# Sliding-window attention and routed experts on one core: transposing k and q on TensorE in place of through DRAM, with the routing rows loaded earlier in a half step

## The chip, the cores and the metric

The kernel runs on one core of one Trainium2 chip. A core has five engines that run their own instruction lists in order and meet at semaphores: TensorE (PE; its weight loads are listed apart as PEld), VectorE (DVE), ScalarE (ACT), GpSimd (POOL) and SyncE (SP). POOL and SP issue the transfers here, which 16 DMA engines carry out. The metric is the device time of one execution in microseconds (us); lower is better.

## The reference

q, k and v have 8 batches of 8 heads of 576 rows of 64 numbers. The attention is causal, looks 128 positions back, and has a bias that grows linearly with the distance (ALiBi). Its output is read as 4608 tokens of 512 numbers and goes through 8 experts, of which every token takes all, weighted by a matrix P that eight rounds of row and column scaling (Sinkhorn) have balanced.

```python
scores = scale * q @ k.T;  scores = where(mask, scores + bias, -1e9)
x = softmax(scores) @ v                      # -> (4608, 512)
P = exp(x @ w_gate - max)                    # (4608, 8), then 8 rounds:
P /= P.sum(1); P /= P.sum(0); P *= N / E
out = sum over e of P[:, e:e+1] * (relu(x @ w1[e]) @ w2[e])
```

## The kernel before, in words

The order of every engine's instructions is written out by hand: each engine executes its part of the program in the order in which the Python code emits it, and nothing is rescheduled.

**Attention (lines 158 to 559).** The unit of work is a block: one batch b and one of five stretches kb of 128 key positions (the fifth has 64). A loop over 40 blocks (line 510) emits, for each block: scores of four heads (`scores`, line 255: matmuls at L280 into the PSUM tile psS, and the exponential on ACT at L291), the gate logits of finished tokens (L358), the turning of a finished block of x (`put_x`, L373 on PE, L382 on DVE), pieces of expert 0's matmuls as filling (`fill`: L129 first layer, L147 second layer), the mask (L301, DVE), then scores of the other four heads, and `attend` for the block before (L333 on PE, L341 and L342 on DVE). The first dozen blocks follow a list of operations (`ORDER`, line 51). psS has one buffer at this stage, so the scores of one half wait for the exponential of the half before.

The scores need q and k with the head dimension on the partitions. There are two ways to that here:
- *By TensorE.* `load_qk` (line 193) loads half of a batch's heads as 96 partitions by 4 by 384 numbers (L208, POOL). `turn` (line 226) reorders it on DVE (L230, 96x1536). `tr_unit` (line 236) makes one of four units: six transposing matmuls of 96x96 (L241) into one PSUM bank psT of the pool "pmm", which has four banks and serves also the filling, the gates and `put_x`; then one copy out of it (L250, 128x576), on ACT for k and on DVE for q. In the block loop, the turns for batch b+1 are made in blocks kb 0 and 2 of batch b, and the units in blocks kb 1 to 4: k's in the first half of the block and q's after the filling in the second half.
- *By DMA.* For the pairs in `by_dma` (line 187: k of batches 4 to 7, q of batches 5 and 7) POOL copies the tensor, cast to 16 bits, to DRAM (L196), and SP transposes it from there into KT or QT (L519), in block kb 1 of the batch before. These pairs have no turns and no units.

**Between (lines 561 to 671).** P is balanced on DVE and POOL while PE works on the rest of expert 0. P's transpose goes to DRAM (PTd, L668).

**Experts 1 to 7 (lines 674 to 1170).** A task is one expert and one group of 512 tokens; there are 63. Each half step h of the loop at line 1017 does the second layer of task h and the first layer of task h+1, both as seven products in place of eight (Strassen), whose sums are on DVE. DVE scales the x of task h+2 by its routing row (`make_xs`, L704) in half step h. The row of a task is read from PTd into 128 partitions, 256 KB, by `load_p` (L696); x is read by `load_x` (L123), 512 KB; both are issued by SP, and both have two buffers. `load_next(h)` (line 1011) issues the row and the x of task h+3, in this order, at the end of half step h. In the half steps of expert 1 (h from 0 to 7) SP also issues two stores (L633, listed at L85) that wait for ACT in the middle of the half step.

Of the kernel before, what the change touches and what calls it, by code (L numbers as in the profile page):

```python
# [9 lines left out]
FP16 = mybir.dt.float16  # L10
# [4 lines left out]
def kernel(  # L15
# [10 lines left out]
    nc = tc.nc  # L26
# [4 lines left out]
    B, H, S, Dh = q.shape  # L31
    HD = H * Dh
# [125 lines left out]
    with (  # L158
# [7 lines left out]
        def new_banks(name: str, n: int):  # L166
# [13 lines left out]
        KTs = [asb.tile([P, NPR, S], FP16, name=f"KT{i}") for i in range(2)]  # L180
        QTs = [asb.tile([P, NPR, S], FP16, name=f"QT{i}") for i in range(2)]
# [1 line left out]

        raw: dict = {}


        by_dma = {("k", b) for b in range(4, B)} | {("q", b) for b in range(5, B, 2)}
        d16 = {
            nb: nc.dram_tensor(f"{nb[0]}16_{nb[1]}", [S, HD], FP16, kind="Internal").ap()
            for nb in sorted(by_dma)  # L190
        }

        def load_qk(b: int):
            for nm, src in (("k", k), ("q", q)):
                if (nm, b) in by_dma:
                    nc.gpsimd.dma_start(  # L196
                        out=d16[nm, b].rearrange("s (h d) -> s h d", d=Dh),
                        in_=src[b].rearrange("h s d -> s h d"),
                    )
            for half in range(2):  # L200
                h0 = 4 * half
                for nm, src in (("k", k), ("q", q)):
                    if (nm, b) in by_dma:
                        continue
                    t = asb.tile(
                        [RP, 4, RT * Dh], FP16, name=f"{nm}f_{b}_{half}", tag="qkf", bufs=6
                    )
                    nc.gpsimd.dma_start(  # L208
                        out=t,
                        in_=src[b, h0 : h0 + 4].rearrange("h (p r) d -> p h (r d)", r=RT),  # L210
                    )
                    raw[(nm, b, half)] = t
# [202 lines left out]
        with tc.manual_schedule():  # L415
            new_banks("aps", 2)
            zw = asb.tile([P, GT], FP16, name="zw")
            nc.vector.memset(zw, 0.0)

            def warm():  # L420

                z = aps.tile([P, GT], FP32, name="psZ", tag="psN")
                nc.tensor.matmul(out=z, lhsT=zw[:, 0:P], rhs=zw)

            nc.sync.dma_start(out=ident, in_=ident_h.ap())
            load_qk(0)
            nc.sync.dma_start(out=rel, in_=rel_h.ap())
            for h in range(H):
                nc.scalar.mul(sid[:, h, :], ident, -float(slopes[h]) / scale)

            def make_mask(h):
                if h < H:
                    nc.scalar.activation(
                        out=maskT[:, h, :], in_=rel, func=AF.Exp, scale=-float(slopes[h])
                    )

            for vsb in vsbs:
                nc.vector.memset(vsb[:, :, :, Dh : Dh + 2], 1.0)
            load_v(0)
            nc.gpsimd.dma_start(  # L440
                out=wg_sb, in_=moe_w_gate.rearrange("(dt p) e -> p dt e", p=P)
            )
            load_qk(1)
            load_w1(0, per, 2)
            load_v(1)
            load_w2(0, per)

            blocks = [(b, kb) for b in range(B) for kb in range(NKB)]
            pts: dict = {}
            groups = 0  # L450
            def finish(i: int):
                b, kb = blocks[i]
                return attend(b, kb, pts[i], pts[i - 1] if kb > 0 else None)

            def finish2(i: int):
                nonlocal groups
                b, kb = blocks[i]
                put_x(b, kb, xsbs.pop(i))
                done = b * S + min(S, (kb + 1) * P)
                while (groups + 1) * GT <= done:  # L460
                    nc.sync.dma_start(
                        out=x_dram(groups), in_=xT[:, :, GT * groups : GT * groups + GT]
                    )
                    if groups in (NHI // 4, NHI // 4 + 1):
                        load_x(f"0_{groups}", groups)
                    add_group(groups)
                    groups += 1
                return done

            xsbs: dict = {}  # L470
            masks: dict = {}

            def op(name: str):

                c, n = name[0], [int(x) for x in name[1:].split(".") if x]
                if c == "B":
                    new_banks(f"aps_{len(masks)}", n[0])
                elif c == "z":
                    warm()
                elif c == "e":  # L480
                    make_mask(n[0])
                elif c == "v":
                    load_v(n[0])
                elif c == "l":
                    load_qk(n[0])
                elif c in "tT":
                    turn(n[0], n[1], "k" if c == "t" else "q")
                elif c in "uU":
                    tr_unit(n[0], "k" if c == "u" else "q", *n[1:])
                elif c == "s":  # L490
                    pt, mask = scores(*blocks[n[0]], n[1])
                    masks[tuple(n)] = mask
                    pts[n[0]] = (*pts.get(n[0], ()), pt)
                elif c == "m":
                    masks[tuple(n)]()
                elif c == "n":
                    xsbs[n[0]] = finish(n[0])
                elif c == "x":
                    return finish2(n[0])
                elif c == "g":  # L500
                    gates((n[0] + 1) * P)
                elif c == "f":
                    moe.pop(0)[1]()
                return 0

            done = 0
            for name in ORDER:
                done = max(done, op(name))
            first_i = max(xsbs, default=-1) + 2
            for i, (b, kb) in enumerate(blocks):  # L510
                if i < first_i:
                    continue
                units = []
                if kb >= 1 and b + 1 < B:
                    units = [(b + 1, n, kb - 1) for n in ("k", "q") if (n, b + 1) not in by_dma]
                if kb == 1:
                    for nm, t in (("k", KTs), ("q", QTs)):
                        if (nm, b + 1) in by_dma:
                            nc.sync.dma_start(  # L519
                                out=t[(b + 1) % 2], in_=d16[nm, b + 1], transpose=True  # L520
                            )
                credit = min(credit + RATE, 6.0) if groups else 0.0
                pt0, mask0 = scores(b, kb, 0)
                gates(done)
                done = finish2(i - 2)
                for u in units[: len(units) // 2]:
                    tr_unit(*u)
                fill(1)
                turning = kb in (0, 2) and b < B - 1
                if turning and ("k", b + 1) not in by_dma:  # L530
                    turn(b + 1, kb // 2, "k")
                mask0()
                pt1, mask1 = scores(b, kb, 1)
                pts[i] = (pt0, pt1)
                xsbs[i - 1] = finish(i - 1)
                mask1()
                fill(2)
                for u in units[len(units) // 2 :]:
                    tr_unit(*u)
                fill(1)  # L540
                if turning and ("q", b + 1) not in by_dma:
                    turn(b + 1, kb // 2, "q")
                if kb == 0 and b + 1 < B:
                    load_v(b + 1)
                if kb == 3 and b + 2 < B:
                    load_qk(b + 2)
            i = len(blocks) - 1
            credit = 1e9
            fill(1)
            xsbs[i] = finish(i)  # L550
            gates(done)
            done = finish2(i - 1)
            fill(1)
            fill(1)
            done, last = finish2(i), done
            gates(last)
            fill(1)
            gates(done)
            fill(1 << 20)
# [7 lines left out]
    with (  # L567
# [17 lines left out]
        for it in range(ITERS):  # L585
# [3 lines left out]
                out=P_sb,  # L589
# [420 lines left out]

        def load_next(h):
            if h + 3 < NT:
                load_p(h + 3)
                load_x(h + 3, tasks[h + 3][1])

        load_next(-1)
        for h in range(NT + 1):
            j = h + 1
            slot = -1

            def extra():
                nonlocal slot
# [178 lines left out]
```

## Time and profile before

| what | value |
|---|---|
| time, median of three runs | 1011.35 us (1010.64, 1011.35, 1013.1) |
| time of the profiled execution | 1010.64 us |
| span of the profiled execution | 1008.9 us (1.7 us less: start and end around the span) |
| PE busy | 988.7 us, 98% of the span |
| PE weight loads busy | 802.6 us, 80% |
| DVE busy | 809.1 us, 80% |
| ACT busy | 642.0 us, 64% |
| POOL busy | 219.1 us, 22% |
| granted TensorE clock, mean | 0.999 |

Batch b of the attention is taken here from the start of its first scores to that of the next batch's: 48.0, 72.0, 94.5, 115.7, 136.8 and 158.0 us are the starts of batches 2 to 7. Expert 0 and the balancing last to about 222 us, and experts 1 to 7 to the end.

How to read it: busy times are sums over instructions that overlap in the engine's pipeline, so a busy PE is not a PE at its peak. A line of the timeline has start, length, engine, source line, operation, output<-inputs, shape and count; lines with a count merge neighbours. What stands in brackets is the engine's idle time before it and the instruction that ended it. In the view of waits a line says who waited for whom, the sum in us, how often, and the longest.

### The profile page before, as it was taken

Reading aid. Unit: us, or ns where it says so; the run is one execution under the profiler, and the core shown is the slowest. Engines: PE = TensorE matmul, PEld = TensorE weight load, DVE = VectorE, ACT = ScalarE, POOL = GpSimd, SP = SyncE. Lnnn points to the kernel's source line nnn. Section 1 sums busy time; section 2 is a strip of 40 time slices with the busy share of each in tenths; the row PEclk is TensorE's granted clock in tenths of the full one; section 3 lists DMA queues with packets and bytes.
Section 4 is the critical chain, followed back from the end, with each engine's and each line's share of the span. In section 5 each row is a group of like instructions: output and inputs, shape, how many; then the busy total and the mean of one; then the engine's idle time right before and its main releaser. Section 6 shows DMA issues by size and latency. Waiting matters only on the chain. (4 is left out here: it accounts for less than half of the span.)

```text
span 1008.9 us, 22248 instructions
## 1 busy us (share of the span) xinstructions
PE 988.7 (98%) x9101; PEld 802.6 (80%) x9101; DVE 809.1 (80%) x1252; ACT 642.0 (64%) x1177; POOL 219.1 (22%) x218
## 2 busy tenths in 40 slices
PE   6999999999999999999999999999999999999997
PEld 4655454458888788888888888888888888888886
DVE  4776665578999898878889988888889988888886
ACT  5866666558999766655656666656566565665652
POOL 7424410201322311111111211111112112222222
PEclk9999999999999999999999999999999999999999
DMA  9999991482987874444446766443438546555546
GB/s 167 198 156 137 139 147 64 102 189 77 228 160 152 180 146 102 104 101 101 101 101 138 140 140 130 95 96 95 95 95 159 117 102 147 145 139 137 136 95 136
DMA packets 163894, 130.87 MB, mean 130 GB/s; under 512 B 85680, under 2 KB 141776, under 8 KB 163792
## 3 DMA queue, kind: packets, MB, share of 16 engines
q0 software_dynamic: 117728, 60.58, 46.3%
q1 hardware_dynamic: 45744, 68.61, 22.8%
q8 instruction: 71, 1.16, 0.5%
q10 hardware_dynamic: 320, 0.26, 0.1%
q14 instruction: 31, 0.25, 0.1%
HBM read 112.90 MB, written 20.20 MB: 132 GB/s over the span
## 5 line engine op out<-in xcount | busy, mean ns | idle before, releaser
L129 PEld LDWEIGHTS <-w1t_122 128*128 128x128 f16 x288 | 25.7, 98 | 26.2 <-issue 0.9
L764 PEld LDWEIGHTS <-w1t_3049 128*128 128x128 f16 x288 | 28.2, 98 | 4.5
L764 PEld LDWEIGHTS <-w1t_3067 128*128 128x128 f16 x288 | 28.1, 98 | 4.6 <-issue 1.2
L764 PEld LDWEIGHTS <-w1t_8191 128*128 128x128 f16 x288 | 28.1, 98 | 4.3 <-issue 0.3
L764 PEld LDWEIGHTS <-w1t_4989 128*128 128x128 f16 x288 | 28.1, 98 | 3.8 <-issue 0.3
L764 PEld LDWEIGHTS <-w1t_7655 128*128 128x128 f16 x288 | 28.2, 98 | 3.6 <-issue 0.3
L764 PEld LDWEIGHTS <-w1t_10591 128*128 128x128 f16 x288 | 28.2, 98 | 3.6 <-issue 0.3
L764 PEld LDWEIGHTS <-w1t_3807 128*128 128x128 f16 x256 | 25.0, 98 | 2.9
L219 POOL DMA_DIRECT2D vsb_79<-in_v_dram x20 | 17.1, 864 | 36.8 <-PE psN_1_1093 L333 7.0
L219 POOL DMA_DIRECT2D vsb_80<-in_v_dram x20 | 16.9, 849 | 29.1 <-PE psT_q_2_2239 L241 4.6
L280 PEld LDWEIGHTS <-KT_76 64*128 64x128 f16 (+1 forms) x160 | 5.5, 96 | 13.8 <-issue 12.5
L280 PEld LDWEIGHTS <-KT_75 64*128 64x128 f16 (+1 forms) x160 | 5.3, 97 | 14.1 <-issue 13.0
L597 POOL PARTITION_ALL_REDUCE ca_sb<-cs_sb x8 | 3.1, 390 | 60.5 <-DVE cs_sb L594 60.5
L639 ACT ACTIVATE acc_lo<-acc_lo,Pe_sb 128x512 f32<-128x512 f32 (+1 forms) x24 | 14.8, 616 | 0.0
L85 POOL DMA_DIRECT2D out_dram<-acc_lo x12 | 13.3, 1498 | 0.0
L358 PEld LDWEIGHTS <-xT 128*128 128x128 f16 x144 | 6.1, 96 | 5.1 <-issue 2.9
L892 POOL DMA_DIRECT2D acc_lo<-st_1_0_3650 x1 | 1.2, 1243 | 34.1 <-ACT st_1_0_3650 L891 34.1
L764 PEld LDWEIGHTS <-ws_2_4125 128*128 128x128 f16 x72 | 7.0, 98 | 1.5 <-issue 0.7
L764 PEld LDWEIGHTS <-ws_1_3369 128*128 128x128 f16 x72 | 7.0, 97 | 1.3
L85 POOL DMA_DIRECT2D out_dram<-acc_hi x6 | 5.7, 1561 | 9.7 <-DVE acc_hi L882 9.7
L919 DVE TENSOR_TENSOR acc_lo<-acc_lo 128x512 f32<-128x512 f32 x12 | 7.7, 682 | 0.0
L764 PEld LDWEIGHTS <-ws_2_3961 128*128 128x128 f16 x72 | 7.0, 98 | 0.8
(4097 smaller groups left out, 3534.1 us busy)
## 6 DMA issues: line engine op xcount, KB each, us to landing
xTd<-xT SPq DMA_DIRECT2D x9, 512.0 KB, 4.9
out_dram<-acc_lo SPq DMA_DIRECT2D x12, 256.0 KB, 5.6
vsb_79<-in_v_dram POOLq DMA_DIRECT2D x16, 128.0 KB, 6.7
vsb_80<-in_v_dram POOLq DMA_DIRECT2D x16, 128.0 KB, 6.6
out_dram<-acc_lo SPq DMA_DIRECT2D x12, 128.0 KB, 4.0
out_dram<-acc_lo POOLq DMA_DIRECT2D x12, 128.0 KB, 7.4
w1t_122<-in_moe_w_dram POOLq DMA_DIRECT2D x2, 512.0 KB, 10.3
w2t_130<-in_moe_w_dram POOLq DMA_DIRECT2D x1, 1024.0 KB, 14.0
```

Source lines behind the costliest of these rows:

```text
L85: eng.dma_start(out=out[t0 : t0 + n, c0:c1], in_=t[n * c : n * c + n], **kw)
L129: nc.tensor.matmul(out=psh, lhsT=w1t[:, dt, P * ft : P * ft + P], rhs=x[:, dt, :], start=(dt == 0), stop=(dt == NDT - 1),)
L219: nc.gpsimd.dma_start(out=vsb[0:nk, kb, :, 0:Dh], in_=v[b, :, k0 : k0 + nk, :].rearrange("h s d -> s h d"),)
L280: nc.tensor.matmul(out=ps[0:nk, hh, jj, 0:nq], lhsT=KT[rows, 2 * half + jj, k0 : k0 + nk], rhs=QT[rows, 2 * half + jj, k0 : k0 + nq], star ...
L358: nc.tensor.matmul(out=psG, lhsT=xT[:, dt, P * blk : P * blk + P], rhs=wg_sb[:, dt, :], start=(dt == 0), stop=(dt == NDT - 1),)
L597: nc.gpsimd.partition_all_reduce(ca_sb, cs_sb, P, bass_isa.ReduceOp.add)
L639: nc.scalar.mul(acc(blk)[:, c], acc(blk)[:, c], Pe_sb[:, 0, blk : blk + 1])
L764: nc.tensor.matmul(out=ps[:, f, :], lhsT=a[:, kt, f0 : f0 + P], rhs=b[:, kt, :], start=(m in (1, 5) and f == 0 and kt == 0), stop=(kt == 1 ...
L892: nc.gpsimd.dma_start(out=quad(self.g, rh, ch), in_=st, accum_op=ALU.add)
L919: tt(out=t, in0=t, in1=quad(g, 1, 1), op=ALU.add)
```

## The change

The change has two parts. First, `by_dma` and its DRAM tensors go away, with the casts to DRAM and the DMA transposes: k of batches 4 to 7 and q of batches 5 and 7 are loaded, turned and transposed as those of the other batches are. Second, `load_p(h + 3)` is called at the beginning of half step h, ahead of everything else in it, and `load_x(h + 3)` stays at its end; ahead of the loop, `load_p(2)` comes behind `load_x` of task 2.

```diff
-        by_dma = {("k", b) for b in range(4, B)} | {("q", b) for b in range(5, B, 2)}
-        d16 = {
-            nb: nc.dram_tensor(f"{nb[0]}16_{nb[1]}", [S, HD], FP16, kind="Internal").ap()
-            for nb in sorted(by_dma)
-        }
...
         def load_qk(b: int):
-            for nm, src in (("k", k), ("q", q)):
-                if (nm, b) in by_dma:
-                    nc.gpsimd.dma_start(
-                        out=d16[nm, b].rearrange("s (h d) -> s h d", d=Dh),
-                        in_=src[b].rearrange("h s d -> s h d"),
-                    )
             for half in range(2):
                 h0 = 4 * half
                 for nm, src in (("k", k), ("q", q)):
-                    if (nm, b) in by_dma:
-                        continue
...
                 if kb >= 1 and b + 1 < B:
-                    units = [(b + 1, n, kb - 1) for n in ("k", "q") if (n, b + 1) not in by_dma]
-                if kb == 1:
-                    for nm, t in (("k", KTs), ("q", QTs)):
-                        if (nm, b + 1) in by_dma:
-                            nc.sync.dma_start(
-                                out=t[(b + 1) % 2], in_=d16[nm, b + 1], transpose=True
-                            )
+                    units = [(b + 1, nm, kb - 1) for nm in ("k", "q")]
...
-                if turning and ("k", b + 1) not in by_dma:
+                if turning:
                     turn(b + 1, kb // 2, "k")
...
-                if turning and ("q", b + 1) not in by_dma:
+                if turning:
                     turn(b + 1, kb // 2, "q")
...
         def load_next(h):
             if h + 3 < NT:
-                load_p(h + 3)
                 load_x(h + 3, tasks[h + 3][1])
 
         load_next(-1)
+        load_p(2)
         for h in range(NT + 1):
             j = h + 1
             slot = -1
+            if h + 3 < NT:
+                load_p(h + 3)
```

## The prediction

> **What bounds the kernel now.** I read the busy time per stage first, then the order of PE's instructions with their starts, then PE's waits, and last the transfers. The windows by batch, for batches 2 to 6 (columns: window and length; busy us and instructions of PE, PEld, DVE, ACT, POOL; clock; DMA):
>
> ```profile
> 48.01:71.97 23.96, 23.75 (x279) 13.63 (x278) 17.83 (x36) 16.98 (x33) 7.77 (x8) 1.00 1.40 149
> 71.97:94.54 22.57, 21.51 (x230) 11.60 (x228) 15.14 (x32) 13.96 (x25) 8.77 (x7) 1.00 1.47 134
> 94.54:115.68 21.14, 19.89 (x207) 10.20 (x206) 12.40 (x26) 13.30 (x24) 7.77 (x8) 1.00 1.52 173
> 115.68:136.80 21.12, 20.79 (x225) 11.25 (x224) 13.47 (x28) 13.91 (x24) 7.89 (x7) 1.00 1.51 133
> 136.80:158.01 21.21, 20.75 (x210) 10.44 (x209) 12.21 (x27) 14.43 (x26) 2.43 (x3) 1.00 0.72 122
> ```
>
> PE is busy nearly throughout at a clock of 1.00, while DVE and ACT are at 58 to 74% and 62 to 71%. Batch 2, in the first line, is the stage as the change makes it everywhere: in it both k and q of batch 3 are transposed on PE. Batches 3 and 5 transpose only q for the next batch, batches 4 and 6 nothing. What PE waits for in batches 3 to 6:
>
> ```profile
> PE psS_3_0_1837 L280 <- ACT pt_2_1_1813 L291: 0.7, 1, 0.7
> PE psS_2_0_1432 L280 <- ACT pt_1_1_1408 L291: 0.7, 1, 0.7
> PE psS_4_0_1902 L280 <- ACT pt_3_1_1873 L291: 0.5, 1, 0.5
> PE psS_3_0_1495 L280 <- ACT pt_2_1_1461 L291: 0.4, 1, 0.4
> PE psXT_3_2329 L373 <- DVE xsb_3_2286 L342: 0.3, 1, 0.3
> ```
>
> No DMA is among them: the DMA transposes and the loads of q and k are hidden today. From 218 us on, PE's whole list of waits is six lines with 1.8 us, of which 0.6 belong to lb_0_1_5060. So both parts of the kernel are bound by the work on PE, and the change puts work on PE.
>
> **Part 1, PE.** k of four batches and q of two, four units each, make 16 + 8 = 24 units: 144 transposing matmuls with as many weight loads. What a unit costs is read from the starts around one, in the timeline of PE:
>
> ```profile
> 59.71 0.38 PE L373 MATMUL psXT_0_1062<-ident,xsb_0_1002 128*128 128x128 f16 x4
> 59.93 0.42 PE L241 MATMUL psT_k_1_1068<-ident,kp_0_904 96*128 96x96 f16 x6
> 60.19 1.03 PE L129 MATMUL psh_1_1_1076<-xT,w1t_122 128*128 128x512 f16 x4
> ...
> 106.61 0.29 PE L333 MATMUL psN_1_1816<-vsb_79,pt_1_1_1752 128*128 128x65 f16 x4
> 107.55 0.34 PE L280 MATMUL psS_3_0_1837<-QT_77,KT_75 64*128 64x192 f16 x4 [0.66 <-ACT pt_2_1_1813 L291]
> ```
>
> The unit's six matmuls show 0.42 us, but the next matmul starts 0.26 us after the first of them; the ends overlap. Others in batch 2 give 0.25, 0.26 and 0.31. Ahead of scores the gap is 0.35, but there any predecessor pays that: a filling of 0.86 us takes 0.95 ahead of scores. So 24 x 0.26 = **+6.2 us** if nothing hides them. A second way, whole batches: 23.96 us of batch 2 hold 12.07 us of filling (8 first-layer pieces of 0.86, 3 second-layer pieces of 1.73) and 11.9 of the rest; batch 6, with the same filling, has 21.21 - 12.07 = 9.1 of the rest. Batch 2 has ten units (two left over from its own q), and one turning of x (0.23) and one gate (0.12) more than batch 6: (11.9 - 9.1 - 0.35) / 10 = 0.24 a unit. Both agree.
>
> The Trainium skill, page "TensorE: Matmul & The Clock Gate", section "Part 4: PE-mode transpose", gives about 275 ns for a 128x128 transpose inside a kernel; 144 of these would be 39.6 us, an estimate by that page. This trace shows 206 ns as the length of one 96x96 transpose, but starts 43 ns apart. The row decides. [...]
>
> **What the waits give back.** The last line above shows a wait in the second half of a block, for an exponential whose end does not depend on what PE does meanwhile. q's unit falls right there. In batch 4 that holds for the two waits of 0.66 and 0.50: two of its four q units are free, -0.5. At the end of batch 6 PE waits 0.15 for scores and then 0.29 for a turned block; the q unit lies ahead of both and is free, -0.25. The waits of batches 3 and 5 have their q unit already; k's units lie in the first half, where nothing is waited for. Together **-0.8**.
>
> **Part 1, DVE and ACT.** DVE gets 12 turns of 0.55 (the rows of L230) and 8 copies of 0.75 (L250): 12.6 us over 86 us of batches 3 to 6, where it is busy 53.2; that makes 72% of about 92. ACT gets 16 copies of 0.64: 10.2 on top of 55.6, also 72%. Batch 2 runs at 74% and 71% with PE waiting 0.2 us in all, for a psT bank whose copy was late (psh_1_3 on QT_78, 0.21). I add that once for each of batches 4 and 6, **+0.4**; its ends are 0 and 16 x 0.21 = 3.4 us. Should DVE or ACT lose their slack, the scores would wait for them at up to the whole 12.6 us.
>
> **Part 1, queues.** POOL loses six casts of 2.2 to 2.8 us and gets twelve loads of 0.67 to 1.2; SP loses six DMA transposes of 2.5 to 4.4 us. The new loads stand where the casts stood, for batch 5 at about 77 us, and are needed in block 0 of batch 4 at about 95; landing took 4.4 to 14.0 us for the like. Issued by about 81, they are there at 89 by the median of 8.0 and just in time by the longest; beyond that the turn, and PE's unit one block later, would be late by the excess. Lighter DMA traffic frees nothing that PE waits for: 0.
>
> **Part 2, the routing rows.** SP works in order. From expert 2 on its list alternates row, x, row, x in both kernels, with the same stores between: the move changes nothing there but semaphore numbers. In expert 1's half steps two stores that wait for ACT stood ahead of the row, so row and x were issued 0.5 us apart, row first. Now the row goes ahead of the stores and x alone behind. The view of DMA issues (KB each, us to landing) shows both cases:
>
> ```profile
> xl_3517<-xTd SPq DMA_DIRECT2D x1, 512.0 KB, 3.5
> ...
> xl_3883<-xTd SPq DMA_DIRECT2D x1, 512.0 KB, 6.8
> ...
> xl_4987<-xTd SPq DMA_DIRECT2D x1, 512.0 KB, 5.9
> ...
> xl_6038<-xTd SPq DMA_DIRECT2D x1, 512.0 KB, 3.3
> ```
>
> Without a row just ahead it is 3.3 to 4.0; with one, 5.7 to 7.7. So x lands about 2 us sooner. Only one x is waited for on the way to a wait of PE: DVE waits 0.49 us for xl_4987 at 337.6, and its sum for lb_0_1_5060 is late by 0.65 at 341.2. That may fall by 0.49: **-0.45**, between 0 and -0.65. A row that now arrives behind its x (task 2) is needed at 241.0 and would be there at about 238: 0, or DVE's wait by the excess. SP's new early row waits for the second L704 of the task two before, which ends at 258.8 for the row of task 5, ahead of the stores at 263.6: nothing is held up.
>
> **Sum.** 6.2 - 0.8 + 0.4 - 0.45 = **+5.35 us**. On the profiled execution's 1010.64 that is 1016.0; its median stands 0.71 higher, and the result will be a median too, so I say **1016.7 us**, 0.5% slower.
>
> **Rivals.**
> *The units vanish in PE's waits* (not slower). PE's idle time in batches 3 to 6 is 1.06 + 1.25 + 0.33 + 0.46 = 3.1 us. If the units swallow all of it, and part 2 the full 1.15 us that PE waits at 334 to 341: 6.2 - 3.1 - 1.15 = +2.0, 1012.6 to 1013.4. It decides if k's units too bring the exponentials forward. Against it: k's units stand in the half that has no waits, and three waits already have a unit in them. 0.12.
> *Late copies hold PE.* psT banks stay taken while DVE or ACT is behind, 0.21 us for each of the 16 units of batches 4 and 6: 3.4 in place of 0.4, +8.3, 1019.0 to 1019.7. For it: one such wait in batch 2; against it: only one. 0.10.
> *x becomes late for DVE.* DVE is 91% busy in expert 1 (77.65 of 85 us), so lost time there can't be made up; 1 us for each of eight half steps makes +13.8, 1025. It needs the early row to slow the x ahead of it; after 353 us rows follow x at once and x lands in 3.3 to 4.0. 0.04.
> *The change frees more than is seen*, by transfers that slow an engine unseen: the DVE copies in question last 0.75 with DMA transposes under way and without. Faster than 1008: 0.02.
>
> The forecast has 0.72. Differences below 0.3%, 3.0 us, can't be told from no change in this kernel: faster 0.02, same 0.12, slower 0.86. The range takes in the units' lower price with the first rival's upper end, and the second rival whole: 1013.0 to 1020.5.
>
> **What would show it.** Right: batch 4 and 6 longer by about 1.6 and 1.8 us, batches 3 and 5 by 1.0; PE's start of expert 0's rest at about 191 in place of 185; waits of 0.66 and 0.50 in batch 4 shrunk to about 0.3; x of expert 1 landing in 3 to 5 us; the same time from there to the end, less 0.5. Wrong: new waits on L250 in PE's list, DVE waiting for a DMA in L230, or half steps of expert 1 longer than 12.2 us.

## The result, and the profile after

The changed kernel takes 1019.47 us (median of 4 runs, 1017.81 to 1020.85); the kernel before, on the same chip, 1011.0 us (4 runs, 1010.1 to 1013.1). The ratio is 1.008, 95% interval 1.0057 to 1.0103: slower by 8.5 us. The forecast was 1016.7, slower by 5.35, with a range of 1013.0 to 1020.5. The direction and the place were right; the size was too small. The time also lies between the 1019.0 and 1019.7 of the rival "late copies hold PE"; this is chance, as the batches below grew by 6.7 us, and experiments 6 and 7 put what the copies cost at 0.9.

The profiled execution of the changed kernel took 1020.1 us (span 1018.3 against 1008.9). The first lines of its page, with busy us, share and count of each engine:

```profile
span 1018.3 us, 22580 instructions
...
PE 993.4 (98%) x9245; PEld 808.4 (79%) x9245; DVE 819.5 (80%) x1272; ACT 650.8 (64%) x1193; POOL 214.2 (21%) x224
```

PE is busy 4.7 us longer than before, DVE 10.4, ACT 8.8, POOL 4.9 less. The spans differ by 9.4 us. By stage this is +2.58 up to the start of batch 2, 0.00 in batch 2, +6.74 in batches 3 to 6, +0.31 from batch 7 to the first matmul of the balancing, and -0.23 from there to the end. (PE's busy time falls by 1.98 in the first stage, in which the clock differed, and grows by 6.66 in batches 3 to 6.) Batches 3 to 6, in the view of windows with the columns of the prediction, and then their sum in the kernel before:

```profile
74.55:98.64 24.09, 22.75 (x254) 12.71 (x253) 16.06 (x34) 16.20 (x29) 7.00 (x9) 1.00 0.82 101
98.64:121.76 23.12, 22.11 (x254) 12.46 (x254) 15.96 (x33) 15.78 (x29) 6.98 (x9) 1.00 0.84 101
121.76:143.91 22.15, 21.81 (x250) 12.26 (x249) 15.09 (x31) 15.97 (x28) 6.11 (x9) 1.00 0.87 104
143.91:167.33 23.42, 22.93 (x259) 12.77 (x258) 15.93 (x34) 16.69 (x30) 2.53 (x3) 1.00 0.36 60
sum 92.78, PE 89.60 PEld 50.20 DVE 63.04 ACT 64.64 POOL 22.62; mean PE 22.40 PEld 12.55 DVE 15.76 ACT 16.16 POOL 5.65
```

```profile
sum 86.04, PE 82.94 PEld 43.49 DVE 53.22 ACT 55.61 POOL 26.87; mean PE 20.73 PEld 10.87 DVE 13.30 ACT 13.90 POOL 6.72
```

The same batches lasted 22.57, 21.14, 21.12 and 21.21 us before, 86.04 in all. They grew by 1.52, 1.98, 1.03 and 2.21, together **6.74 us**. PE's busy time grew from 82.94 to 89.60 in them, by 6.66, and its idle time stayed (3.10 before, 3.18 after). So the added time is PE's, stage for stage where the change puts work. What fills the idle time did change, as PE's waits show (who waited for whom; sum, times, longest, in us; 74.5 to 168 us; the lines are those of the changed kernel, whose L226, L235 and L276 are L241, L250 and L291 before):

```profile
PE psS_2_0_1444 L265 <- ACT pt_1_1_1420 L276: 0.7, 1, 0.7
PE psS_3_0_1517 L265 <- ACT pt_2_1_1483 L276: 0.4, 1, 0.4
PE psS_3_0_1919 L265 <- ACT pt_2_1_1885 L276: 0.4, 1, 0.4
PE psy_11_1947 L147 <- ACT P_sb L350: 0.3, 1, 0.3
PE psh_2_0_1545 L129 <- ACT P_sb L350: 0.3, 1, 0.3
PE psXT_3_2487 L358 <- DVE xsb_3_2444 L327: 0.3, 1, 0.3
PE psS_4_0_2399 L265 <- ACT pt_3_1_2359 L276: 0.2, 1, 0.2
PE psS_4_0_2003 L265 <- ACT pt_3_1_1963 L276: 0.2, 1, 0.2
PE psh_4_5_2650 L129 <- DVE QT_78 L235: 0.2, 1, 0.2
```

The two score waits of batch 4, 0.66 and 0.50 before, have shrunk to 0.40 (psS_3_0_1919) and 0.24 (psS_4_0_2003) by the unit that now stands ahead of each, about as forecast. In the place of what went stand three waits that were not there: filling (psy, psh) that waits for a bank of the pool "pmm", 0.28 + 0.28 + 0.24 us. The last of them waits for a copy of L250 (L235 here); the prediction had named new waits on L250 as a sign of being wrong, and had also put two of them, of 0.21 each, into its sum. One came. The timeline of PE around one of them, and around a unit without a wait (start, length, line, operation, tiles, shape, count, idle before):

```profile
89.34 0.38 PE L358 MATMUL psXT_1_1530<-ident,xsb_1_1485 128*128 128x128 f16 x4
89.57 0.42 PE L226 MATMUL psT_k_2_1536<-ident,kp_1_1475 96*128 96x96 f16 x6
90.26 1.02 PE L129 MATMUL psh_2_0_1545<-xT,w1t_122 128*128 128x512 f16 x4 [0.28 <-ACT P_sb L350]
...
108.68 0.42 PE L226 MATMUL psT_k_1_1859<-ident,kp_0_1718 96*128 96x96 f16 x6
108.93 1.03 PE L147 MATMUL psy_10_1867<-w2t_130,hT_2_1544 128*128 128x512 f16 x4
```

The k unit shown without a wait takes 0.25 from start to start; the forecast had 0.26. With the bank wait, 0.69 pass; 0.28 of these are the wait and 0.41 are not, so the unit ahead of a wait is also dearer than 0.26.

The medians differ by 8.5 (5.8 to 10.4 by the interval of the ratio), batches 3 to 6 by 6.74. In the profiled execution nearly all of the rest lies ahead of batch 2, which begins at 50.6 us against 48.0 before. It arises in batch 1, in which the change does nothing. PE's timeline there:

```profile
41.47 0.66 PE L226 MATMUL psT_q_1_709<-ident,qp_0_680 96*128 96x96 f16 x6 [3.72 <-DVE qp_0_680 L215]
...
42.83 1.91 PE L129 MATMUL psh_0_6_731<-xT,w1t_122 128*128 128x512 f16 x4
```

The same place before:

```profile
40.41 0.43 PE L241 MATMUL psT_q_1_709<-ident,qp_0_680 96*128 96x96 f16 x6
...
41.16 1.03 PE L129 MATMUL psh_0_6_731<-xT,w1t_122 128*128 128x512 f16 x4
```

In the changed kernel's profile PE waits 3.72 us for the turned q of batch 2, whose load lands late, and then runs at half speed (1.91 us where such a piece takes 1.03). In the profile of before PE came to full speed later, came to this place later, and did not wait: batch 1 began at 29.0 there and at 26.2 here. The kernel before has the same weak place; the experiments take it out of both.

### The profile page after: what moved, and what is told of

It reads as the page before. It is cut to its first block, busy times and chain, and to the rows that moved or that the text cites. A ratio compares the mean times of both kernels' runs of the same rounds, so it can differ in the third digit from the quotient of the medians.

```text
span 1018.3 us, 22580 instructions
## 1 busy us (share of the span) xinstructions
PE 993.4 (98%) x9245; PEld 808.4 (79%) x9245; DVE 819.5 (80%) x1272; ACT 650.8 (64%) x1193; POOL 214.2 (21%) x224
## 3 DMA queue, kind: packets, MB, share of 16 engines
q8 instruction: 72, 1.18, 0.5%
## 5 line engine op out<-in xcount | busy, mean ns | idle before, releaser
L129 PEld LDWEIGHTS <-w1t_122 128*128 128x128 f16 x288 | 26.1, 98 | 27.2 <-issue 2.4
L743 PEld LDWEIGHTS <-w1t_3277 128*128 128x128 f16 x288 | 28.2, 98 | 4.5
L743 PEld LDWEIGHTS <-w1t_3295 128*128 128x128 f16 x288 | 28.1, 98 | 4.5 <-issue 1.0
L743 PEld LDWEIGHTS <-w1t_8421 128*128 128x128 f16 x288 | 28.1, 98 | 4.3 <-issue 0.3
L743 PEld LDWEIGHTS <-w1t_5219 128*128 128x128 f16 x288 | 28.1, 98 | 3.7 <-issue 0.3
L743 PEld LDWEIGHTS <-w1t_10821 128*128 128x128 f16 x288 | 28.2, 98 | 3.6 <-issue 0.3
L743 PEld LDWEIGHTS <-w1t_7885 128*128 128x128 f16 x288 | 28.2, 98 | 3.6 <-issue 0.3
L743 PEld LDWEIGHTS <-w1t_4037 128*128 128x128 f16 x256 | 25.0, 98 | 2.9
L743 PEld LDWEIGHTS <-ws_2_4355 128*128 128x128 f16 x72 | 7.0, 98 | 1.5 <-issue 0.7
L743 PEld LDWEIGHTS <-ws_1_3597 128*128 128x128 f16 x72 | 7.0, 97 | 1.3
L226 PE MATMUL psT_k_0_138<-ident,kp_0_133 96*128 96x96 f16 x6 | 0.7, 278 | 7.3 <-DVE kp_0_133 L215 7.3
```

The costliest lines, as they stand in the source:

```text
L129: nc.tensor.matmul(out=psh, lhsT=w1t[:, dt, P * ft : P * ft + P], rhs=x[:, dt, :], start=(dt == 0), stop=(dt == NDT - 1),)
L226: nc.tensor.matmul(out=psT[:, r, :], lhsT=tt[:, r, 2 * Dh * jj : 2 * Dh * jj + 2 * Dh], rhs=ident[0:RP, 0:RP], is_transpose=True, start=(r ...
L743: nc.tensor.matmul(out=ps[:, f, :], lhsT=a[:, kt, f0 : f0 + P], rhs=b[:, kt, :], start=(m in (1, 5) and f == 0 and kt == 0), stop=(kt == 1 ...
```

## The experiments

The theory at this point: PE bounds the attention, the 24 units cost their time on PE wherever PE is not waiting, and a small part is bank waits; the start of the program draws 1 to 3 us in either kernel. The rivals are those of the prediction (units vanish in waits; late copies are most of it), and part 2 as a cause.

**1. Part 1 alone.** The changed kernel with the row loaded at the end again:

```diff
-        load_p(2)
         for h in range(NT + 1):
...
-            if h + 3 < NT:
-                load_p(h + 3)
...
         def load_next(h):
             if h + 3 < NT:
+                load_p(h + 3)
                 load_x(h + 3, tasks[h + 3][1])
```

> Part 1 alone: all q and k on TensorE, the routing rows loaded at the end of the half step as before. Theory: the 24 units cost 0.26 us each and late copies some 1 us more; batches 3 to 6 grow by 6.5 to 7.0 us in sum (1.5, 2.0, 1.0, 2.2 as in the profile after), so the kernel takes 6.5 to 9 us more than before, the rest being what the first 50 us draw. Rival, that the early rows cost time too: 2 us or more below the changed kernel.

Measured: 1019.6 us (6 runs), the kernel before 1012.41 on the same chip (17 runs), ratio 1.0074 (1.0058 to 1.0089). Batches 3 to 6 last 24.10, 23.11, 22.17 and 23.42 us, as with the whole change. So the loss is part 1's. (The profiled execution is the slowest of the six, 1023.22; a late wait in expert 1, shown in the last section, is in it too.)

**2. Part 2 alone.** The kernel before with the row loaded at the beginning (the same lines, the other way).

> Part 2 alone: the DMA transposes as before, the rows at the beginning of the half step. Theory: x of expert 1 lands in 3.2 to 4.2 us in most half steps in place of 5.7 to 7.7, PE's wait at lb_0_1 shrinks from 0.65 to about 0.5, the time is that of before within 1 us (-0.2). Rival, that the early rows are a cost: 1.5 us or more above before.

Measured: 1011.16 us (11 runs), ratio 0.9991 (0.9983 to 1.0). The wait at lb_0_1, which the forecast expected to lose 0.45, is 0.64 in its profile (0.65 before), and the time from the balancing's first matmul to the end is 796.04 us in both. Part 2 alone changes nothing that can be told from zero.

**3. and 4. The wait at the start removed from both kernels.** Expert 0's second-layer weights, 1 MB, are loaded behind q and k of batch 2 and not ahead of them:

```diff
             load_v(1)
-            load_w2(0, per)
...
                 elif c == "l":
                     load_qk(n[0])
+                    if n[0] == 2:
+                        load_w2(0, per)
```

> The kernel before with expert 0's second weights (1 MB read as 2 MB) loaded behind batch 2's q and k in place of ahead of them. Theory: batch 2's q and k land in about 7 to 9 us in place of 13 to 14, no turn waits for them, and the first 50 us get shorter or stay: 0 to 3 us below before, with a smaller spread. Rival, that these loads are late for another reason: same time as before, same landing times.

> The changed kernel with the same edit. Theory, that part of the 8.5 us is a start that happened to be worse: PE's wait of 3.7 us for batch 2's q and the half clock behind it are gone, 1.5 to 4 us below the changed kernel, and 6.3 to 7.2 us above e3_before_w2late. Rival, that the change itself makes the start slower: 8 us or more above e3_before_w2late.

Measured: the kernel before with it 1009.65 us (5 runs; ratio to before 0.997, 0.9958 to 0.9982), the changed kernel with it 1016.14 (5 runs; 1.0034, 1.0021 to 1.0047). The wait of 3.72 is in neither profile. The start is still tight: in the first of the two profiles PE waits 1.24 us for the weights themselves, in batch 1, and in the six profiles with this edit in which batch 2 begins before 47 us it lasts 24.4 to 25.2 us in place of 23.96. Batches 3 to 6 keep their lengths (22.58, 21.14, 21.12, 21.21 and 24.10, 23.12, 22.16, 23.42), and the difference between the two medians is **6.5 us** (runs of 1008.3 to 1010.7 and of 1015.5 to 1017.3): the growth of the batches, within the spread of the runs, and not the 8 or more of the rival that the change makes the start slower. The next four kernels build on the second of these. Each was run once, and its whole time (1020.31, 1017.84, 1014.02 and 1014.79 us, the kernel before 1013.59 beside them) holds the draw of the start too; the lengths of the batches come back within 0.02 us, and these are compared. The sum of batches 3 to 6 in the base:

```profile
sum 92.80, PE 89.62 PEld 50.22 DVE 63.07 ACT 64.65 POOL 22.61; mean PE 22.40 PEld 12.55 DVE 15.77 ACT 16.16 POOL 5.65
```

**5. The added units' transposes made twice.**

```diff
-            for r in range(RT):
+            for r in [*range(RT)] * (2 if (nm == "k" and b >= 4) or b in (5, 7) else 1):
```

> The changed kernel with expert 0's second-layer weights loaded later, in which the 24 added units make their six transposes twice (the same result written twice; one copy). PE's cost by itself. Batches 3 to 6 last 92.80 us without the doubling (24.10, 23.12, 22.16, 23.42). Theory (PE has no room there, six matmuls cost 0.26): 24 x 0.26 = 6.2, less what still falls in the waits that are left (0.4 to 0.6): 98.2 to 99.0 in the sum, batches 3 and 5 longer by 1.0, batches 4 and 6 by 1.6 to 2.1. Rival (units vanish in PE's waits): under 95. Rival (the added time is late copies and not PE): under 94, as the copies are the same.

```profile
71.41:96.22 24.81, 23.72 (x279) 13.69 (x278) 16.06 (x34) 16.31 (x29) 6.97 (x9) 1.00 0.78 98
96.22:120.62 24.40, 24.14 (x304) 14.47 (x302) 16.04 (x33) 16.14 (x29) 6.97 (x9) 1.00 0.82 97
120.62:143.74 23.12, 22.79 (x274) 13.23 (x273) 15.02 (x31) 15.95 (x28) 6.11 (x9) 1.00 0.82 100
143.74:168.72 24.98, 24.72 (x308) 14.66 (x306) 16.20 (x35) 17.09 (x30) 2.53 (x3) 1.00 0.34 57
sum 97.31, PE 95.37 PEld 56.04 DVE 63.33 ACT 65.48 POOL 22.59; mean PE 23.84 PEld 14.01 DVE 15.83 ACT 16.37 POOL 5.65
```

In the sum's line PE's busy time is 95.37 against 89.62: +5.75, that is 0.24 for six transposes. The batches last 97.31, +4.51, since PE's idle time falls from 3.18 to 1.94. Both rivals (under 95, under 94) are out. The theory's figure was missed too, by 0.9 us, as more went into waits than it said: all three bank waits and three of six score waits (68 to 172 us) are gone from this profile. Time that PE spends ahead of a bank wait is not lost.

**6. and 7. The added units' copies out of psT made twice, and left out.** In the second, k of batches 4 to 7 and q of batches 5 and 7 are those of an earlier batch.

```diff
-            copy(
+            for _ in range(2 if (nm == "k" and b >= 4) or b in (5, 7) else 1):
+                copy(
```

```diff
-            copy(
+            if not ((nm == "k" and b >= 4) or b in (5, 7)):
+                copy(
```

> The same base; the 24 added units' copies out of psT are made twice, 16 on ACT and 8 on DVE, PE's work unchanged. ACT gets 10.2 us more and DVE 6 in batches 3 to 6. Theory (of the 6.8 us by which batches 3 to 6 grew, 5.4 are PE's own and some 1.3 are waits behind copies): the waits for banks grow, 92.80 becomes 94 to 96, with more waits of PE for P_sb's exponentials and k's copies on ACT. Rival (late copies hold PE, 0.21 each and more): every unit waits now, above 97. Rival (all 6.8 us are PE's own and copies cost nothing): 92.8 to 93.2.

> The same base; the 24 added units are transposed on PE and not copied out of psT, so that k of batches 4 to 7 and q of batches 5 and 7 are those of an earlier batch (left out: 24 copies, 16 on ACT and 8 on DVE). Theory: what the copies cost comes off, some 1.3 us: 92.80 becomes 91.3 to 91.8, that is PE's own 5.4 us over 86.04. Rival (all of it PE's own): 92.6 to 92.8. Rival (late copies are most of it): under 90.

The sums of batches 3 to 6, first with the copies twice, then without them:

```profile
sum 95.30, PE 90.03 PEld 50.53 DVE 68.13 ACT 74.31 POOL 22.59; mean PE 22.51 PEld 12.63 DVE 17.03 ACT 18.58 POOL 5.65
```

```profile
sum 91.87, PE 89.20 PEld 50.01 DVE 58.46 ACT 55.94 POOL 22.59; mean PE 22.30 PEld 12.50 DVE 14.61 ACT 13.98 POOL 5.65
```

PE executes the same work in both (busy 90.03 and 89.20, against 89.62; part of the difference is that a unit ahead of a wait takes 0.42 in place of 0.26). Twice the copies give +2.50, none give -0.93: the first in the theory's range, the second 0.07 short of it; 0.44 of the 0.93 are batch 4's, 0.49 batch 6's, and batches 3 and 5 do not move at all. So the copies cost about 0.9 us, in the two batches where all eight units are new, and not the 8.3 of the rival "late copies hold PE". In the second kernel PE's waits (69 to 172 us) hold one bank wait still:

```profile
PE psS L266 <- ACT pt L277: 2.2, 6, 0.7
PE psXT L359 <- DVE xsb L328: 0.5, 2, 0.3
PE psh L129 <- ACT P_sb L351: 0.3, 1, 0.3
```

That is the wait of batch 3. It does not come from the added copies, which are left out here. The q unit, the gate logits, the turned x and the k unit take a bank each, which makes four, the whole pool; the filling behind them, which was the fourth here before the change, is now the fifth and needs one of these back. It starts at 85.63 us, when the gates' exponential P_sb, which stands on ACT behind the scores' exponential of 0.81 us, has just ended:

```profile
84.70 0.81 ACT L277 ACTIVATE pt<-psS 128x768 f16<-128x768 f32 x1 [0.43 <-PE psS L266]
85.40 0.17 ACT L351 ACTIVATE P_sb<-psG 128x8 f32<-128x8 f32 x1
```

The copy of this q unit, for batch 4, is no added one and is still made. In batch 4, with the same five in the same order, the q unit is an added one, its copy is left out, and there the filling no longer waits: it starts at 108.65, ahead of the gates' exponential (108.87).

```profile
108.65 1.89 PE L147 MATMUL psy<-w2t,hT 128*128 128x512 f16 x8
...
108.87 0.17 ACT L351 ACTIVATE P_sb<-psG 128x8 f32<-128x8 f32 x1
```

So the filling does not always get the gates' bank; what decides which of the four it gets was not traced.

**8. k's units in the second half of a block,** ahead of q's, with k's turning behind them:

```diff
-                for u in units[: len(units) // 2]:
+                late = b >= 3
+                for u in units[: 0 if late else len(units) // 2]:
...
-                if turning:
+                if turning and not late:
                     turn(b + 1, kb // 2, "k")
...
-                for u in units[len(units) // 2 :]:
+                for u in units[0 if late else len(units) // 2 :]:
                     tr_unit(*u)
                 fill(1)
+                if turning and late:
+                    turn(b + 1, kb // 2, "k")
```

> The same base; for the turned blocks of batches 4 to 7 k's unit and its turning are moved from the first half of a block to the second, ahead of q's unit, where PE waits for exponentials. Theory (units are free exactly where PE waits): the waits that are left in the second half (0.4, 0.3, 0.2) are covered by k's units, and the bank waits behind ACT's exponentials in the first half go: 92.80 becomes 91.5 to 92.3. Rival (a unit costs its 0.26 wherever it stands): 92.7 to 92.9. Rival (two units one after the other wait for a bank): 93.3 to 95.

```profile
sum 91.01, PE 89.93 PEld 50.07 DVE 64.10 ACT 63.19 POOL 22.61; mean PE 22.48 PEld 12.52 DVE 16.03 ACT 15.80 POOL 5.65
```

```profile
PE psS L265 <- ACT pt L276: 0.7, 2, 0.4
```

The second line is PE's whole list of waits from 68 to 172 us. The batches shrink by 1.79 us, more than the 0.5 to 1.3 expected: the bank waits are gone, the score waits fall from 2.2 to 0.7, and every k unit now takes 0.25 to 0.26 from start to start (in the first half they took 0.30 on average, waits not counted). PE still has the same work; what the place of k's units, and of the turnings that moved with them, cost is 1.8 of the 6.76.

**9. and 10. The other direction.** The kernel of experiment 3 with q of batches 4 and 6 by DMA too, so that PE transposes neither from batch 4 on; and the same with part 2.

```diff
-        by_dma = {("k", b) for b in range(4, B)} | {("q", b) for b in range(5, B, 2)}
+        by_dma = {(n, b) for n in ("k", "q") for b in range(4, B)}
```

> The other direction: the kernel before with expert 0's second-layer weights loaded later, and q of batches 4 and 6 too brought by DMA, so that from batch 4 on PE transposes nothing of q and k. Eight units of q fewer in batches 3 and 5, which last 22.58 and 21.12 us now. Theory (PE's work bounds, a unit is worth 0.26 where nothing is waited for and nothing where PE waits next for an exponential): two or three of the eight stand ahead of such a wait, so 5 or 6 x 0.26 = 1.3 to 1.6 us less, 1008.0 to 1008.4 against 1009.65, and about 0.997 x 0.9985 = 0.9955 of the kernel before. Rival (the DMA transposes become late: two of them, for k and q, one after the other on SP in every batch): scores wait for KT or QT, not faster than 1009.65. Rival (a unit costs its 0.26 in whatever place): 2.1 us less, 1007.5.

> The same with the routing row loaded at the beginning of a half step, the second part of the change. Theory: 0 to 0.7 us less than without it, as the x of expert 1 that PE waited for by way of DVE lands sooner and nothing else moves. Rival (the early row slows the x ahead of it): over 1 us more, half steps of expert 1 longer than 12.2 us.

Measured: 1009.03 us (11 runs; ratio to before 0.9971, 0.996 to 0.9981) and 1009.13 us (11 runs; 0.9971, 0.9958 to 0.9984). Batches 3 to 6 of the first:

```profile
71.92:93.99 22.07, 20.49 (x206) 10.41 (x205) 12.52 (x27) 13.82 (x24) 8.68 (x8) 1.00 1.65 160
93.99:115.18 21.19, 19.93 (x205) 10.24 (x205) 11.65 (x25) 13.35 (x24) 8.67 (x7) 1.00 1.78 174
115.18:135.88 20.70, 19.91 (x201) 10.24 (x201) 10.79 (x23) 13.77 (x24) 7.79 (x6) 1.00 1.68 163
135.88:157.12 21.24, 20.75 (x208) 10.44 (x208) 11.66 (x26) 14.43 (x26) 2.45 (x3) 1.00 0.73 122
sum 85.20, PE 81.08 PEld 41.33 DVE 46.62 ACT 55.38 POOL 27.58; mean PE 20.27 PEld 10.33 DVE 11.65 ACT 13.84 POOL 6.90
```

Batches 3 and 5 lose 0.51 and 0.42 us where 1.3 to 1.6 was expected for both. PE's work falls by 1.86 (82.94 to 81.08), but its idle time grows from 3.11 to 4.12, in waits for exponentials (2.9 to 3.9 us from 60 to 175). At 0.26 each, 0.93 us is the worth of 3.6 units: some four of eight q units, not two or three, had been free. Batch 7 is 0.42 longer (27.47 against 27.05), with a bank wait of 0.3 that was not there, which takes back nearly half; why it came there was not tried. Part 2 on top is again nothing. Both are 0.3% faster than the kernel before. But so is experiment 3, with the same ratio of 0.997: what the removal of the q units adds can't be told from zero, and the gain is that of the later load of the weights.

## Why the prediction came out as it did

The forecast for batches 3 to 6 was 5.8 us (6.2 - 0.8 + 0.4); 6.74 were measured. (Its signs of being right, 1.0, 1.6, 1.0 and 1.8 us for the four batches, make 5.4: they leave out the +0.4. The batches grew by 1.52, 1.98, 1.03 and 2.21.) Term by term, from the starts in the profile after:

- **The price of a unit, +6.2.** Too small for k. The sixteen k units take 0.25 to 0.42 to the next start, without waits; their sum is 4.83, 0.30 each, not 0.26. The forecast took the price from one gap of 0.26 and noted others of up to 0.31 without using them. That is 0.7 us. Experiment 5 confirms that PE is where it is paid.
- **What the waits give back, -0.8.** Right in the sum, and nearly in the places. The eight q units cost 8 x 0.26 = 2.08 at full price, and what is left of the growth for them (batch 4: 1.98 - 1.18 - 0.28 = 0.52; batch 6: 2.21 - 1.31 - 0.24 = 0.66) is 1.18: 0.9 came back, 0.5 of it in batch 4. At the end of batch 6 the wait of 0.15 for scores is gone, but that for the turned block, which the forecast also took as free, is still 0.26 (0.29 before). k's units did not vanish anywhere in the first half, as said; experiment 8 shows that part of their cost does so in the second.
- **Bank waits, +0.4.** Measured 0.80: 0.52 in batches 4 and 6, where it was expected, and 0.28 in batch 3, which the forecast did not name. By the profile only that of batch 6 ends with a late copy; the other two end with the gates' exponential, since a k unit more leaves the filling behind it without a free bank (experiment 7). With what the copies delay besides, they cost 0.93. It was the right mechanism with one cause missing; the rival of 16 x 0.21 was not what happened.
- **Part 2, -0.45.** Wrong in size: nothing. The x of expert 1 does land sooner in six of nine half steps (3.2 to 4.1 us, before mostly 5.7 to 7.7), but the PE wait that was to fall is 0.48 in the profile after and 0.64 in that of part 2 alone, against 0.65. It varies by itself: without part 2 it is 2.34 in experiment 1's profile and under 0.4 in experiment 9's. From the balancing to the end the profile after is 0.23 us shorter than that of before (795.81 against 796.04), that of part 2 alone not at all.
- **DVE, POOL and SP.** No new wait for a turn, a load or a transfer appears in batches 3 to 6, with DVE at 68% and ACT at 70% (sum line: 63.04 and 64.64 of 92.78). The queues were costed right, at nothing.
- **The rest, 8.5 - 6.7.** The forecast took the profiled execution of before, in which PE came to full speed late and the wait of 3.7 us was absent, as the rule for both kernels. What each median holds of this draw was not measured, and 6.7 lies within the interval of the 8.5. Experiments 3 and 4, without that wait, give 6.5, so nothing asks for a further cost of the change.

## What to carry to other kernels

Where one engine is busy throughout at full clock, a few tenths of a microsecond of added work are paid in full, unless they stand directly ahead of a wait whose end does not depend on that engine: the same 24 units cost 6.76 us in one place of the block and 4.97 in another. Take the price of an inserted piece from the mean of all start-to-start gaps in the place where it will stand, and count every buffer that it takes from a shared pool: what comes after it may have to wait for one that is freed later. An engine's idle time in a profile may be cover that some piece of work already makes use of, as the removal of the q units showed.

## What the runs showed of the hardware

- **After a wait of 2.34 us PE ran at half clock for some 3 us.** After 3.72 us of waiting in the profile after, the granted clock is 0.50 in the next 3.3 us. In experiment 1 a wait of 2.34 us (at lb_0_1, for an x that landed late) was enough. After waits of 1.24 (experiment 3) and 1.05 (experiment 5) it stayed at 1.00, and from 20 to 1000 us no other stretch of 3 us in the twelve profiles is under 0.97. Windows and PE's timeline of that kernel:

```profile
350.50:352.80 2.30, 0.73 (x7) 0.66 (x7) 1.61 (x3) 0.00 (x0) 0.00 (x0) 1.00 1.14 209
352.80:356.00 3.20, 3.20 (x18) 2.02 (x17) 2.66 (x4) 1.71 (x3) 0.00 (x0) 0.60 1.09 230
356.00:359.00 3.00, 3.00 (x18) 1.65 (x17) 0.59 (x2) 1.67 (x3) 0.61 (x1) 0.86 0.56 215
```

```profile
352.07 0.60 PE L743 MATMUL lb<-xl,w1t 128*128 128x256 f16 x4 [2.34 <-DVE lc L783]
352.50 0.60 PE L743 MATMUL lc<-xl,ws 128*128 128x256 f16 x4
352.94 0.60 PE L850 MATMUL M<-T,S 128*128 128x256 f16 x4
353.45 1.01 PE L743 MATMUL lb<-xd,w1t 128*128 128x256 f16 x4
...
355.10 1.88 PE L129 MATMUL psh<-xl,w1t 128*128 128x512 f16 x4
```

The first three groups of matmuls after the wait still run at full speed (0.60), and the slow ones begin 1.4 us after its end; after the wait of 3.72 they began at once. The Trainium skill, page "TensorE: Matmul & The Clock Gate", section "Why this matters for your kernels", asks for no gaps of PE over some 3 us between bursts; here 2.34 us in one piece were too many, and the measurement decides.

- **When PE runs at full speed at the start varies by 7 us or more.** The same four matmuls in the profile before and in the one after:

```profile
15.84 1.04 PE L269 MATMUL psS_1_0_236<-rel,sid 128*128 128x256 f16 x4
```

```profile
14.55 0.61 PE L254 MATMUL psS_1_0_236<-rel,sid 128*128 128x256 f16 x4
```

Before, such groups take 0.84 to 1.05 up to 20 us and 0.60 from 21 us on; after, 1.05 at 9.6 us and 0.60 from 13.7 us on. The granted clock in the windows is 1.00 in all of this time in these two profiles, so the column does not show it; the lengths do. (In experiment 5's profile it does: 0.63 and 0.52 from 13 to 17 us, with no wait there over 0.8 us.) With it moves the start of batch 1 (25.6 to 29.1 us in the profiles of this study). In a kernel whose loads are just in time early full speed can cost more than it gains: with it batch 2 began at 50.6, without it at 48.0; with the weights loaded later, 45.2 to 46.8 and 48.0, though batch 2 was then 0.4 to 1.3 us longer.
